# A dynamic convolution and a maxout layer in one kernel: first batch sooner, weights by halves, and w1 turned by the crossbar

## The chip, the cores and the metric

The kernel runs on one core of a Trainium2 chip. The metric is the device time of one execution in microseconds (us), lower is better. A time is some 1.8 us above the span of the profile (from the first to the last instruction): the profiled execution of the kernel before has a span of 429.9 us and a time of 431.71. TensorE does the matmuls; VectorE, ScalarE and GpSimd do the rest; SyncE, ScalarE and GpSimd issue transfers, which all run on the same 16 DMA engines.

## The reference

```python
# x (8, 4160, 192), weight_gen (8, 4160, 8 heads, 7 taps), w1, w2 (192, 1024), w_out (1024, 192), all fp32
w = exp(weight_gen - max);  w = w / (sum over the 7 taps + 1e-9)
conv[b, s, h, :] = sum over k of w[b, s, h, k] * x_padded[b, s + k, h, :]     # 24 features a head
out = maximum(conv @ w1, conv @ w2) @ w_out                                    # 33280 tokens
```

The kernel uses max(a, b) = a + relu(b - a). So it needs wd = w2 - w1 for the hidden product, and w10 = w1 @ w_out once, to add conv @ w10 to the output.

## The kernel before

The tokens lie as 128 partitions x 260 columns of 192 features. Batches of 16 columns go through ScalarE (exponentials) and VectorE (seven tap products, then adds). The result must be transposed for TensorE, in units of 4 or 8 columns. A unit of four columns in the opening is summed and transposed on TensorE (`sum_transpose`: 6 blocks x 7 taps, 42 matmuls); later units are added on VectorE and transposed by the DMA crossbar (`transpose`). The hidden product runs in groups of two tiles at first and of three tiles from tile 12 on.

```python
def transpose(u):                        # VectorE has added; the crossbar transposes
    ...
    nc.sync.dma_start_transpose(out=yt[...], in_=y_ts[b][:, o * D:(o + n) * D])

def sum_transpose(u):                    # TensorE adds the seven taps and transposes
    ...
    for k in range(nb):
        for t in range(K):
            nc.tensor.matmul(yps[:, k * P:(k + 1) * P], lhsT=m_ts[b][...], rhs=ident,
                             start=(t == 0), stop=(t == K - 1), skip_group_check=True)
    nc.scalar.copy(out=yt[:, 0:nb * P], in_=yps[:, 0:nb * P])

# opening (cut): four whole weight loads on one queue, then
load_x(0, 4, 4); load_x(0, 8, 4); ...    # GpSimd, behind the landing of w1's first piece
keep_warm(110)                           # filler matmuls
w1_transposed()                          # 24 transposes on TensorE
keep_warm(6)
sum_transpose(0)
...
tensor_tensor(out=wd["E"], ...)          # VectorE: 1024 features at once, with all three copies
mul(0, 4); red(1); mul(0, 8)
hidden(0); ln(1); hidden(1)
sum_transpose(1)
...                                      # pw: the product w10, 24 matmuls
# and by groups: sum_transpose(2) to (5), transpose(6) on
```

The softmax here doesn't subtract the row's maximum and nothing guards it: scores larger than these inputs give would overflow.

Of the kernel before, what the change touches and what calls it, by code (L numbers as in the profile page):

```python
# [23 lines left out]
def kernel(  # L24
# [107 lines left out]
    def ln(b):  # L132
        nc.scalar.activation(out=s_ts[b], in_=s_ts[b], func=AF.Ln)

    def shift(b):
        TH = BATCHES[b][1] * H
        nc.vector.tensor_tensor(
            out=_sub(wg_ts[b], 0, [[K, TH], [1, K]]),
            in0=_sub(wg_ts[b], 0, [[K, TH], [1, K]]),
            in1=_sub(s_ts.pop(b), 0, [[1, TH], [0, K]]), op=ALU.subtract,  # L140
        )
# [169 lines left out]
    for t0, n in GROUPS:  # L311
        most = 2 if len(OUTS) < 10 or len(OUTS[-1]) == 4 else 4
        OUTS.append([])
        while len(OUTS[-1]) < most and c < NT:
            u = column(c)[0]
            if TILES.index((u, 0)) + UNITS[u][2] > t0:
                break
            OUTS[-1] += [c, c + 1]
            c += 2
    OUTS.append(list(range(c, NT)))  # L320
    NU = len(UNITS)

# [14 lines left out]
    def stretch(g):  # L337

        if g < len(GROUPS):
            t0, n = GROUPS[g]  # L340
            for t in range(t0, t0 + n):
                for f in chunks(t)[0]:
                    for j in range(2):
                        hid_rest(t, f, j, t == t0 + n - 1)
        for k in range(0, len(OUTS[g]), 4):
            if g == len(GROUPS) and k < 8:
                tag, w = ("ab", 2048) if k == 0 else ("c", 1024)
                tile_, at = ps[tag].tile([P, w], FP32, name="op_" + tag, tag=tag), 0
            else:
                tile_, at = ps["r" if "r" in ps else "o"].tile([P, 1024], FP32, name="op_ps", tag="op"), 0  # L350
            for c in OUTS[g][k:k + 4]:
                op_at[c // 2] = tile_, at + (c - OUTS[g][k]) // 2 * D
                out_rest(c, c - OUTS[g][k] < 2)
# [25 lines left out]
    with tc.tile_pool(name="pstage", bufs=1) as pstage:  # L379
# [17 lines left out]
        for wi, wsrc in enumerate((moe_w1, moe_w2)):  # L397
            for kind, r0, nr in (("E", 0, P), ("T", P, 64)):
                nc.sync.dma_start(
                    out=ws[kind, wi],  # L400
                    in_=bass.AP(tensor=wsrc.tensor, offset=r0 * F, ap=[[F, nr], [1, F]]),
                )
# [15 lines left out]
        weights(0, 0)  # L418
        nc.scalar.copy(out=xb_ts[0][:, PAD * D:(PAD + 4) * D], in_=xs[:, PAD * D:])  # L419
# [3 lines left out]
        for kind in "ET":  # L423
            nc.scalar.copy(out=w1[kind], in_=ws[kind, 0])
        for o in (4, 8, 12):
            weights(0, o)

        nc.gpsimd.tensor_copy(out=gate, in_=ws["E", 0][:, 0:1])
        load_x(0, 4, 4)
        load_x(0, 8, 4)  # L430
        nc.gpsimd.dma_start(
# [3 lines left out]
        load_x(0, 12, 4)  # L435
# [6 lines left out]
        tp = ps["o"].tile([P, 1024], FP32, name="tp", tag="op")  # L442
        tpb = tp[:, :].bitcast(BF16)

        def w1_transposed():

            for fi in range(FCH):
                for at, kind, nr in ((0, "E", P), (P + 64, "E", 64), (P, "T", 64)):
                    nc.tensor.matmul(  # L449
                        tpb[:, fi * 256 + at:fi * 256 + at + nr],  # L450
                        lhsT=w1[kind][0:nr, fi * P:(fi + 1) * P],
                        rhs=ident[0:nr, 0:nr], is_transpose=True, skip_group_check=True,
                    )
# [3 lines left out]
        def keep_warm(times):  # L457

            for _ in range(times):
# [3 lines left out]
        keep_warm(110)  # L463
        w1_transposed()
        nc.scalar.copy(out=w1t[:, 0:1024], in_=tpb[:, 0:1024])
        keep_warm(6)
        sum_transpose(0)
        nc.scalar.copy(out=w1t[:, 1024:2048], in_=tpb[:, 1024:2048])
        exp_sum(1)
        keep_warm(18)  # L470

        nc.vector.tensor_tensor(out=wd["E"], in0=ws["E", 1], in1=ws["E", 0], op=ALU.subtract)
        nc.vector.tensor_copy(out=wd["R"][64:P, :], in_=wd["E"][0:64, :])
        nc.vector.tensor_copy(out=wd["O"][0:64, :], in_=wd["E"][64:P, :])
        nc.vector.tensor_tensor(out=wd["R"][0:64, :], in0=ws["T", 1], in1=ws["T", 0],
                                op=ALU.subtract)
        nc.vector.tensor_copy(out=wd["O"][64:P, :], in_=wd["R"][0:64, :])
        mul(0, 4)
        red(1)
        mul(0, 8)  # L480


        hidden(0)
        ln(1)
        hidden(1)
        sum_transpose(1)
        shift(1)
        weights(1, 0)
        weights(1, 4)
        mul(0, 12)  # L490


        pw = ps["o"].tile([P, 1024], FP32, name="pw", tag="op")
        for k in range(3):
            for fi in range(FCH):
                nc.tensor.matmul(  # L496
                    pw[:, k * 256:k * 256 + D],
                    lhsT=w1t[:, fi * 256 + 64 * k:fi * 256 + 64 * k + P],
                    rhs=wo[:, fi * D:(fi + 1) * D],
                    start=(fi == 0), stop=(fi == FCH - 1), skip_group_check=True,  # L500
                )
        nc.scalar.copy(out=_sub(w10, 0, [[D, 3], [1, D]]), in_=_sub(pw, 0, [[256, 3], [1, D]]))
# [4 lines left out]

    def first_of_1():
        m_ts[1] = m_ts[0]
        mul(1, 0)  # L510
        load_x(2, 0, 16)
        load_wg(4, nc.gpsimd)

    def rest_of_1():
        shift(2)
        mul(1, 8)
        load_wg(5, nc.gpsimd)
        load_x(3, 0, 16)
        red(3)
        adds(1, 8)  # L520
# [4 lines left out]
        2: (lambda: (first_of_1(), exp_sum(2), sum_transpose(2)), lambda: weights(1, 8)),  # L525
        3: (lambda: (red(2), ln(2), mul(1, 4), exp_sum(3), sum_transpose(3)), rest_of_1),
        4: (lambda: sum_transpose(4), lambda: weights(2, 0)),
        5: (lambda: (ln(3), sum_transpose(5)), lambda: (exp_sum(4), transpose(6))),
# [3 lines left out]
    def extra(t):  # L532
# [4 lines left out]
        if s == 0 and b + 1 < NB:  # L537

            c = b + 1
            if c + 1 < NB:  # L540
                shift(c + 1)
            if c + 2 < NB:
                red(c + 2)
            for o, _ in pieces(c):
                mul(c, o)
                adds(c, o)
            if b + 5 < NB:
                load_wg(b + 5, nc.gpsimd)
            if b + 3 < NB:
                load_x(b + 3, 0, BATCHES[b + 3][1])  # L550
        if k == 2 and 6 < u + 1 < NU:
            transpose(u + 1)
        if b + 2 < NB:
            for o, at in zip((o for o, _ in pieces(b + 2)), (6, 9)):
                if s == at:
                    weights(b + 2, o)
        if s == 3 and b + 3 < NB:
            ln(b + 3)
        if s == 0 and b + 4 < NB:
            exp_sum(b + 4)  # L560

    for g in range(2, len(OUTS)):
        if GROUPS[min(g, len(GROUPS) - 1)][1] == 3 and "c" not in ps:
            later_ps()
        hidden(g)
# [7 lines left out]
        for k in range(0, len(OUTS[g]), 4):  # L573
            now = OUTS[g][k:k + 4]
# [38 lines left out]
```

## Time and profile before

| kernel before | |
|---|---|
| time, median of 3 | 431.97 us (431.97 to 432.0) |
| span, granted clock | 429.9 us, 1.000 |
| TensorE busy | 420.8 us, 98% |
| VectorE, ScalarE busy | 378.8 us (88%), 351.5 us (82%) |
| first useful hidden matmul | 17.38 us |
| first group of three tiles | 47.82 us |
| last copy of outputs starts | 425.39 us |

The three last rows cut the span into opening, first stretch, steady part and tail; a change in one of them is read from how far the next row moves. TensorE's waits before, from the waits view (line and tensor, what ended the wait, us in total, times, the longest), show how little there was to lose after the start:

```profile
PE hdp L228 <- ACT rd_t L247: 1.0, 1, 1.0
PE op_ps L266 <- ACT o_t L296: 0.4, 1, 0.4
```

After the start, one relu and one copy are waited for, once each, and a second relu for 0.2 us; no DMA is. The list of DMA issues of the same kernel (KB left out for a transpose; median us from issue to landing):

```profile
yt<-y_t SPq DMA_TRANSPOSE x30, 4.5
```

### The profile page before, as it was taken

The page shows a single profiled execution, that of the slowest core. Times are in us where ns is not written, and L with a number is a line of the kernel's source. Part 1 is how long each engine was busy: PE and PEld are TensorE (multiplying, and loading weights), DVE is VectorE, ACT ScalarE, POOL GpSimd, SP SyncE. Part 2 cuts the span into 40 slices and gives each one's busy share as a digit, 9 for nine tenths or more (in the row PEclk, how much of TensorE's full clock was granted, in tenths as well). Part 3 has the DMA queues.
Part 4 walks back from the last instruction along what each step waited for, and adds up shares of the span by engine and source line. Part 5 has one row for each costly group of instructions (what it writes and reads, how often), then busy time and mean ns, then how long its engine had stood idle before and what let it go on. Part 6 is the DMA issues. An engine that isn't in the chain of part 4 may idle for free.

```text
span 429.9 us, 9266 instructions
## 1 busy us (share of the span) xinstructions
PE 420.8 (98%) x4186; PEld 302.8 (70%) x4186; DVE 378.8 (88%) x170; ACT 351.5 (82%) x351; POOL 29.8 (7%) x61
## 2 busy tenths in 40 slices
PE   7999999999999999999999999999999999999995
PEld 7699886767677676676666766667767677676785
DVE  4998999999999999999999999999999999992000
ACT  6777898888889888897988888888878887777762
POOL 2221001010000101010100101010000000000000
PEclk9999999999999999999999999999999999999999
DMA  8984837667482858576392948558565736433112
GB/s 266 206 184 173 176 103 147 161 153 212 121 231 50 211 149 210 126 166 199 50 311 78 208 121 215 114 118 215 131 139 164 148 102 157 104 107 104 75 75 110
DMA packets 59047, 65.45 MB, mean 152 GB/s; under 512 B 48865, under 2 KB 49633, under 8 KB 59008
## 3 DMA queue, kind: packets, MB, share of 16 engines
q0 software_dynamic: 6400, 24.30, 25.7%
q1 hardware_dynamic: 47280, 15.00, 19.0%
q10 hardware_dynamic: 5328, 25.56, 14.8%
q8 instruction: 32, 0.52, 0.5%
q14 instruction: 7, 0.06, 0.0%
HBM read 35.96 MB, written 25.56 MB: 143 GB/s over the span
## 4 chain that ended last, share of the span: by engine, by line
PE 95%; ACT 4%; issue 0%; DVE 0%; ACTq 0%; POOL 0%; POOLq 0%
PE op_ps L283 38%; PE hd L228 26%; PE hd L238 14%; PE op_ps L273 5%; PE yps L199 3%; PE op_ps L266 2%; PE warm L460 2%; ACT rd_t L247 2%; PE hdp L228 1%; PE hdp L238 1%; ACT e_t L125 1%; PE op_c L283 1%; PE op_ab L283 1%; PE tp L449 1%; ACT o_t L296 0%; PE pw L496 0%
## 5 line engine op out<-in xcount | busy, mean ns | idle before, releaser
L247 ACT ACTIVATE rd_t<-hd 128x2048 bf16<-128x2048 f32 (+1 forms) x166 | 230.8, 1443 | 34.1 <-PE hd L238 33.7
L283 PE MATMUL op_ps<-wo,rd_t 128*128 128x192 bf16 x2016 | 194.2, 246 | 0.0
L159 DVE TENSOR_TENSOR m_t<-xb_t,en_t 128x10752 bf16<-128x10752 bf16 (+1 forms) x36 | 187.3, 5206 | 1.5 <-ACT xb_t L419 1.4
L283 PEld LDWEIGHTS <-rd_t 128*128 128x128 bf16 x2080 | 175.6, 98 | 9.2
L228 PE MATMUL hd<-yt,wdE 128*128 128x512 bf16 (+1 forms) x264 | 96.5, 369 | 0.2 <-ACT rd_t L247 0.2
L228 PE MATMUL hd<-yt,wdO 128*128 128x512 bf16 (+1 forms) x264 | 95.5, 366 | 0.0
L177 DVE TENSOR_TENSOR m_t<-m_t 128x4608 bf16<-128x4608 bf16 (+1 forms) x30 | 75.5, 2517 | 1.0
L296 ACT COPY o_t<-op_ps 128x768 f32<-128x768 f32 (+1 forms) x87 | 54.5, 626 | 20.0 <-PE op_ps L283 19.8
L238 PE MATMUL hd<-yt,wdR 64*128 64x512 bf16 (+1 forms) x528 | 68.0, 366 | 0.0
L273 PE MATMUL op_ps<-w,yt 128*128 128x192 bf16 x252 | 62.0, 246 | 0.0
L178 DVE TENSOR_TENSOR m_t<-m_t 128x3072 bf16<-128x3072 bf16 (+1 forms) x30 | 51.9, 1731 | 1.0
L238 PEld LDWEIGHTS <-wdR 64*128 64x128 bf16 x576 | 20.9, 94 | 44.9 <-issue 35.3
L228 PEld LDWEIGHTS <-wdE 128*128 128x128 bf16 x288 | 28.0, 97 | 28.9 <-issue 19.3
L228 PEld LDWEIGHTS <-wdO 128*128 128x128 bf16 x288 | 28.3, 98 | 11.3 <-issue 1.5
L148 ACT ACTIVATE en_t<-wg_t 128x896 bf16<-128x896 f32 (+1 forms) x36 | 34.1, 955 | 2.1 <-ACT o_t L296 2.1
L273 PEld LDWEIGHTS <-yt 128*128 128x128 bf16 x260 | 25.4, 98 | 9.3 <-issue 0.2
L113 POOL DMA_DIRECT2D xb_t<-in_x_dram x20 | 10.8, 544 | 292.5 <-DVE m_t L159 292.5
L179 DVE TENSOR_TENSOR y_t<-m_t 128x1536 bf16<-128x1536 bf16 (+1 forms) x30 | 28.3, 945 | 1.0
L266 PE MATMUL op_ps<-w,yt 64*128 64x192 bf16 x252 | 24.6, 243 | 0.4 <-ACT o_t L296 0.4
L266 PEld LDWEIGHTS <-yt 64*128 64x128 bf16 x260 | 12.7, 94 | 14.6 <-issue 0.7
L130 DVE TENSOR_REDUCE sum_t<-e_t 128x128 f32<-128x896 f32 (+1 forms) x17 | 17.7, 1039 | 3.2 <-ACT e_t L125 3.0
L125 ACT ACTIVATE e_t<-wg_t 128x896 f32<-128x896 f32 (+1 forms) x17 | 15.6, 919 | 4.9 <-ACT o_t L296 2.5
(55 smaller groups left out, 158.2 us busy)
## 6 DMA issues: line engine op xcount, KB each, us to landing
out_dram<-o_t ACTq DMA_DIRECT2D x29, 768.0 KB, 3.3
xb_t<-in_x_dram POOLq DMA_DIRECT2D x14, 768.0 KB, 7.4
wg_t<-in_weight_gen_dram POOLq DMA_DIRECT2D x14, 448.0 KB, 8.0
xb_t<-xb_t POOLq DMA_DIRECT2D x16, 288.0 KB, 8.0
out_dram<-o_t ACTq DMA_DIRECT2D x6, 384.0 KB, 3.7
wg_t<-in_weight_gen_dram SPq DMA_DIRECT2D x2, 448.0 KB, 6.5
xb_t<-in_x_dram POOLq DMA_DIRECT2D x4, 192.0 KB, 6.4
xb_t<-in_x_dram POOLq DMA_DIRECT2D x2, 384.0 KB, 7.6
```

Of the source, the lines that this page charges most:

```text
L148: nc.scalar.activation(out=_sub(en_ts[b], o * WGC * 2, [[2 * N, K], [2, N], [1, 2]]), in_=_sub(wg_ts[b], o * WGC, [[1, K], [K, N], [0, 2]] ...
L159: nc.vector.tensor_tensor(out=m_ts[b][:, K * o * D:K * (o + n) * D], in0=_sub(xb_ts[b], o * D, [[D, K], [1, n * D]]), in1=_sub(en_ts[b], o ...
L177: nc.vector.tensor_tensor(out=taps(0, 1, 3), in0=taps(0, 1, 3), in1=taps(3, 1, 3), op=ALU.add)
L178: nc.vector.tensor_tensor(out=taps(0, 2, 2), in0=taps(0, 2, 2), in1=taps(1, 5, 2), op=ALU.add)
L179: nc.vector.tensor_tensor(out=y_ts[b][:, o * D:(o + w) * D], in0=taps(0, 1, 1), in1=taps(2, 1, 1), op=ALU.add)
L228: nc.tensor.matmul(hid_out(t, f, j), lhsT=wd[kind][:, f * P:(f + 1) * P], rhs=_sub(yt_ts[u], 2 * j * P, [[3 * P, w // P], [1, P]]), start= ...
L238: nc.tensor.matmul(hid_out(t, f, j), lhsT=wd["R"][r, f * P:(f + 1) * P], rhs=_sub(yt_ts[u][r, :], P, [[3 * P, w // P], [1, P]]), start=fir ...
L247: nc.scalar.activation(out=rd[:, k * 1024:(k + n) * 1024], in_=hd[:, at:at + n * 1024], func=AF.Relu)
L266: nc.tensor.matmul(op_out(c), lhsT=yt_ts[u][r, (3 * i + 1) * P:(3 * i + 2) * P], rhs=w10[r, 2 * D:3 * D], start=first, stop=False, skip_gr ...
L273: nc.tensor.matmul(op_out(c), lhsT=yt_ts[u][:, (3 * i + 2 * j) * P:(3 * i + 2 * j + 1) * P], rhs=w10[:, j * D:(j + 1) * D], start=False, s ...
L283: nc.tensor.matmul(op_out(c), lhsT=rd[:, k * 1024 + at:k * 1024 + at + P], rhs=wo[:, f * D:(f + 1) * D], start=False, stop=(f == FCH - 1), ...
L296: nc.scalar.copy(out=_sub(o_t[0], (k + 2 * q) % 24 * D, [[2 * D, w], [D, 2], [1, D]]), in_=_sub(tile_, at + q * D, [[D, w], [512, 2], [1, ...
```

## The change

Its intent: let hidden work begin earlier, by loading and subtracting half of the features first and by taking the 24 w1 transposes off TensorE (the crossbar does them later, just for w10); and sum five units instead of six on TensorE. The order of VectorE's and ScalarE's work in the first groups, the filler, the steady part's order and the tail (last columns as 4, 2, 2) change with it. Its core:

```diff
+        HF = F // 2
+        def load_w(h):
             for kind, r0, nr in (("E", 0, P), ("T", P, 64)):
+                for wi, wsrc in enumerate((moe_w1, moe_w2)):
+                    nc.sync.dma_start(out=ws[kind, wi][:, h * HF:(h + 1) * HF], in_=...)
+        load_w(0)
+        load_w(1)
 ...
-        nc.gpsimd.tensor_copy(out=gate, in_=ws["E", 0][:, 0:1])
+        nc.gpsimd.tensor_copy(out=gate, in_=wg_ts[0][:, 0:1])
         load_x(0, 4, 4)
+        nc.gpsimd.tensor_copy(out=gate[0:64, :], in_=ws["T", 1][:, 0:1])
         load_x(0, 8, 4)
 ...
         def w1_transposed():
-            for fi in range(FCH):
-                for at, kind, nr in ((0, "E", P), (P + 64, "E", 64), (P, "T", 64)):
-                    nc.tensor.matmul(tpb[...], lhsT=w1[kind][...], rhs=ident[...], is_transpose=True, ...)
+            for at, kind, nr in ((0, "E", P), (P + 64, "E", 64), (P, "T", 64)):
+                nc.sync.dma_start_transpose(
+                    out=_sub(w1t, at, [[256, FCH], [1, nr]]), in_=w1[kind][0:nr, :])
 ...
+        w_diff(0); sum_transpose(0); keep_warm(14); w_diff(1); mul(0, 4)
+        hidden(0)
+        nc.scalar.copy(out=w1["E"], in_=ws["E", 0])
+        mul(0, 8); sum_transpose(1); mul(0, 12)
+        nc.vector.tensor_copy(out=w1["T"], in_=ws["T", 0])
+        w1_transposed()
+        hidden(1)
 ...
+        hidden(2)
+        ...                      # mul(1, 0), sum_transpose(2), load_x(2, ...), load_wg(4, ...)
+        adds(1, 4); transpose(5)
+        hidden(3); w10_product(); sum_transpose(3)
```

## The prediction

> **What bounds the kernel now.** I read the page's chain first, because it says which engine has to become faster for the end to move.
>
> ```profile
> ## 4 chain that ended last, share of the span: by engine, by line
> PE 95%; ACT 4%; issue 0%; DVE 0%; ACTq 0%; POOL 0%; POOLq 0%
> ```
>
> The chain is TensorE almost throughout. So I cut the span into stretches and asked for each engine's busy time in each (columns: stretch, its length, then busy time and instruction count of PE, PEld, DVE, ACT, POOL, the granted clock, the DMA share and GB/s).
>
> ```profile
> 3.00:11.20 8.20, 8.18 (x112) 8.08 (x112) 4.05 (x3) 5.64 (x8) 2.20 (x5) 1.00 1.04 331
> 11.20:17.38 6.18, 6.18 (x91) 5.32 (x90) 6.04 (x7) 3.37 (x6) 1.00 (x2) 1.00 1.26 224
> 17.38:47.82 30.44, 29.45 (x414) 26.11 (x411) 28.73 (x14) 24.04 (x32) 5.37 (x10) 1.00 0.71 173
> 47.82:400.00 352.18, 351.63 (x3304) 242.73 (x3303) 338.33 (x144) 301.81 (x291) 19.76 (x37) 1.00 0.60 151
> ```
>
> From 47.82 us on, where the groups of three tiles begin, TensorE is idle for 0.55 us of 352: nothing can be won there unless matmuls go. Between 17.38 (the first useful hidden matmul) and 47.82 it is idle for 1.0 us of 30.4. Before 17.38 it looks busy too, but most of that is filler. So a gain must come from three places: a start before 17.38, fewer matmuls before 47.82, or the tail. The chain in order of time (start, length, what) shows the start:
>
> ```profile
> 3.02 8.19 PE warm L460 x110
> 11.20 2.51 PE tp L449 x24
> 13.71 0.44 PE warm L460 x6
> 14.15 2.36 PE yps L199 x42
> 16.53 0.80 ACT yt L205
> 17.33 0.91 ACT w1t L468
> 18.25 0.85 ACT e_t L125
> 19.10 0.92 ACT rd_t L247
> ```
>
> The first unit's summing transpose (yps, 42 matmuls) ends at 16.5, ScalarE copies it, hidden work starts at 17.38, and the second group then waits because ScalarE still does a w1 copy and the next exp before its relu. What the 14.15 itself waits for is on VectorE (timeline: start, length, engine, line, operation):
>
> ```profile
> 9.33 2.96 DVE L159 TENSOR_TENSOR m_t<-xb_t,en_t 128x5376 bf16<-128x5376 bf16 x1 [1.40 <-ACT xb_t L419]
> 12.21 1.22 DVE L472 TENSOR_TENSOR wdE<-ws1E,ws0E 128x1024 bf16<-128x1024 f32 x1
> 14.35 1.22 DVE L475 TENSOR_TENSOR wdR<-ws1T,ws0T 64x1024 bf16<-64x1024 f32 x1
> 16.05 2.96 DVE L159 TENSOR_TENSOR m_t<-xb_t,en_t 128x5376 bf16<-128x5376 bf16 x1
> ```
>
> The product of the first four columns ends at 12.3, yet its summing waits until 14.15 behind the 24 w1 transposes on TensorE. The tail, from the timeline:
>
> ```profile
> 424.53 0.82 PE L283 MATMUL op_c<-wo,rd_t 128*128 128x192 bf16 x8
> 425.39 0.80 ACT L296 COPY o_t<-op_c 128x768 f32<-128x768 f32 x1 [2.17 <-PE op_c L283]
> 426.22 0.82 ACTq L303 DMA_DIRECT2D out_dram<-o_t  x2
> ```
>
> After the last matmul come a copy of four columns (0.80), two output issues (0.82) and the landing.
>
> **What the Trainium skill says.** "TensorE: Matmul & The Clock Gate", section "Back-to-back issue gap", gives N/2.4 + 2.5 ns between warm matmuls, 55.8 ns for 128 columns, but about 81 ns in a real stream with weight loads. The trace decides for the first: 42 summing matmuls take 2.35 us, 56.0 ns each, so a whole unit's summing costs TensorE 2.35 us. The same page, "What's actually happening", says an idle window of some 3.4 us halves the clock; the trace grants 1.00 everywhere, and the new filler has to keep gaps shorter than that. "VectorE: DVE Perf Modes", "The perf-mode tier table", has fp32 tensor_tensor at 1 element a cycle and an fp32 copy at 2; with its (N+151)/0.96 the 1024-wide subtraction should take 1.22 us, exactly the trace's, so I take 0.69 us for a half of 512 as an estimate, and some 0.56 us for the 768-wide copy that moves to VectorE. "DMA: Bandwidth & Descriptors", "Issuing engines are not separate DMA queues", says that all queues share the 16 DMA engines; the trace agrees as far as it goes: a DMA share of about 1.0 or more until 17.4 us, so moving a load ahead only delays another.
>
> **The change part by part.**
>
> *Start.* VectorE's first shift ends at 7.93 as now. The x cast goes to VectorE (about 0.6, to 8.5) and the first weights are done at 8.57 on ScalarE, so the first product runs about 8.65 to 11.6, 0.7 us earlier. TensorE no longer transposes w1 there. Its filler (40, then 40 pairs on half the rows, which overlap, then 15) ends by my estimate between 10 and 12, so summing runs 11.65 to 14.05 instead of 14.15 to 16.5. VectorE meanwhile subtracts half the features: 0.69 for E to 12.3, 0.69 for R to 12.9. The three half-width copies are now ScalarE's, about 0.6 each by its 0.54 us spacing for 448 elements: they end at about 14.1. The weight bytes are no limit: the first half is 0.79 MB where the whole is 1.57, and even the second tensor of the old order had landed by 12.2. ScalarE's yt copy then runs to 14.95, hidden work starts at about 15.1: **2.3 us earlier**. Only tiles with features of the first half are in the first group, so the second half's subtractions (to about 14.5) and copies (14.95 to 16.7) are off this path.
>
> *Five units instead of six on TensorE.* Minus 42 matmuls, **2.35 us**. VectorE takes over the adds of a four-column unit: half of 2.55 + 1.76 + 0.96, some 2.6 us, and a DMA transpose (4.5 us median to landing). It is needed by tile 20, near 50 us, and lands by my walk near 42.
>
> *w1 by the crossbar.* The 24 transposes stood in time that had no useful work for TensorE, so removing them is already in the start. What is added is a path: ScalarE casts w1E after the first relus (about 18.5 to 19.5), VectorE casts w1T after four products (14.5 + 3 x 2.9 = 23.3, to 23.9), then landing. With 4.5 us it is there at 28.5; the product w10 comes up at about 28.3 and needs the T part only after its first eight matmuls (0.66 us). So nearly no wait, or up to 3 us if the transpose is slow.
>
> *New waits between 15.1 and group six.* Walking the order of the instructions: after hidden group 0 (1.7 us, to 16.8) the next sum waits for the product of columns 4 to 7, which ends at about 17.4: 0.7. Groups 1 and 2 wait for relus, 0.25 and 0.3. ScalarE then stands at the logarithm of batch 1, whose sum waits for VectorE's products until about 24.9, so relus of group 2 run 25.2 to 27.1 and group 3 waits some 0.45. w10's wait 0.3. Together 2.0 to 2.7 us, where before it was 1.0: **1.3 us given back**. Starting from 29.4 of useful work, 15.1 + 29.4 - 2.35 + 2.35 = 44.5 for the start of the three-tile groups, against 47.82: 3.3 earlier.
>
> *Steady state.* Same matmuls, so the same 9.01 us per six tiles (in the chain, the first hidden matmuls of every second group are 9.01 us apart). VectorE's sixteen-column batch takes 24.1 us against TensorE's 24.04, so it must not fall behind. In the old trace the first eight-column transpose is issued at 48.5 and needed at about 66; in the new one I find about 49.4 and 62. The lead shrinks from some 13 to 8 us after the 4.5 us landing, and stays positive.
>
> *Tail.* The last eight columns leave as 4, 2 and 2: a copy of two columns (0.48 instead of 0.80) and one issue instead of two (0.4 less). **0.7 us.**
>
> Sum: -2.3 - 2.35 + 1.3 - 0.7 = -4.05 us, so 431.97 - 4.05 = 427.9 us, a ratio of 0.991.
>
> **The rivals.** First, VectorE takes over as the bound: it is 88% busy, has no idle time after 50 us, and gets 2.6 us of adds while TensorE comes 3.3 us earlier. For it speaks the near equality 24.1 to 24.04; against it the 8 us of lead. If it held, TensorE would lose what exceeds the lead, and the time would be 429 to 431. Second, w1's crossbar path or the bunching on ScalarE costs more than I walked: a w1t landing of 7.7 us (the slowest DMA transpose of the old trace) makes w10 wait 2.9 more, and the time 430.5. Third, the waits were tuned away and the gaps before group six stay at 1 us: then 426.6. Fourth, the loads bound the start, with the second x piece now asked for before the weights: a first half 1.5 us late would stop the subtractions and give 429.
>
> **Range and chances.** The three sizes that I trust (2.3, 2.35, 0.7) sum to 5.35, so 426.6 is about the best, and I take 0.4 off for the roundness of the walk: 426.2. The rivals reach 430.5; I cut the range just under the last, at 430.3. The 2% mark lies at 423.3, beyond everything that I can add up, and slower needs several microseconds of new waits twice over: 2% faster, 97% same, 1% slower.
>
> **What would show it.** Right: hidden matmuls start near 15.1; five yps blocks of 42; the three-tile groups start near 44.5; no wait of TensorE on yt after that; the last copy is 0.48 us with one issue behind it. Wrong: a TensorE wait on a w1t or yt transpose, a VectorE wait for ScalarE's logarithm in the steady part, a granted clock under 1.00 after the pause before the first sum, or hidden work that starts after 16.

## The result, and the profile after

| | before | after |
|---|---|---|
| time, median | 431.99 us (431.97 to 433.07, 4 runs) | 446.06 us (443.69 to 456.43, 4 runs) |
| fast runs | all | 443.69, 444.69, 447.44 |
| span, clock of the profiled run | 429.9 us, 1.000 | 445.6 us, 0.975 |
| first useful hidden matmul | 17.38 | 15.24 |
| first group of three tiles | 47.82 | 64.88 |
| last copy starts, end of span | 425.39, 429.9 | 441.94, 445.6 |

The ratio is 1.0301, with a 95% interval of 1.0242 to 1.036: 3% slower, where a gain of 1% was predicted. Ratios here are the mean time of one kernel's fast runs over that of the other's of the same rounds, so not quite the ratio of the medians that I quote. The run of 456.43 us (clock 0.966) isn't used for the ratio; it does stand in the median and range of the table (the median of the three fast runs is 444.69). The trace is of the run of 447.44 us, the slowest of the three.

The chain that ended last, by engine:

```profile
PE 88%; DMA 7%; ACT 3%; DVE 1%; issue 0%; POOL 0%; DVEq 0%
```

DMA, absent from the list of before, now carries 7% of the path, some 31 of 445.6 us. The stretches (columns as in the prediction: stretch, length, busy time and count of PE, PEld, DVE, ACT, POOL, granted clock, DMA share, GB/s) say where:

```profile
3.00:15.24 12.24, 10.91 (x192) 10.41 (x193) 8.18 (x8) 7.23 (x12) 3.92 (x7) 1.00 1.05 277
15.24:64.88 49.64, 32.77 (x368) 27.70 (x368) 31.21 (x16) 24.84 (x33) 5.38 (x10) 0.79 0.87 125
64.88:417.00 352.12, 351.92 (x3310) 243.48 (x3310) 340.73 (x146) 301.35 (x292) 19.78 (x37) 1.00 0.64 152
```

The start came earlier, as intended, and the steady part is as full as before (TensorE idle 0.2 us of 352). All the loss is in the stretch between: 49.64 us long instead of 30.44, with TensorE idle for 16.87 us of it, and its clock at 0.79. TensorE's waits name three of them:

```profile
PE pw L519 <- DMA w1t<-w1T: 6.6, 1, 6.6
PE pw L519 <- DMA wg_t<-in_weight_gen_dram: 6.2, 1, 6.2
PE yps L197 <- DVE m_t L157: 4.7, 2, 3.5
```

`pw` is the product w10. The first of its waits to end is put down to a weight_gen load, which w10 doesn't read. No such load lands near 38.6 us, where the matmul starts, but the first transpose of w1E does (20.02 + 18.56 = 38.58), and the view of w1t puts a 6.5 us wait of the weight load down to it; so w1t is what was waited for. What these waits do to the work behind them is in TensorE's timeline (start, length, operation, count, wait ahead of it and its releaser):

```profile
20.40 4.15 PE L197 MATMUL yps<-ident,m_t 128*128 128x128 bf16 x42 [3.48 <-DVE m_t L157]
...
38.62 1.46 PE L519 MATMUL pw<-wo,w1t 128*128 128x192 bf16 x8 [6.22 <-DMA wg_t<-in_weight_gen_dram]
46.66 2.74 PE L519 MATMUL pw<-wo,w1t 128*128 128x192 bf16 x16 [6.58 <-DMA w1t<-w1T]
49.20 3.58 PE L197 MATMUL yps<-ident,m_t 128*128 128x128 bf16 x42
```

The waits are 3.48, 6.22 and 6.58 us. And the sum of 42 blocks behind a wait takes 4.15 or 3.58 us where it took 2.51 in every place before; the 24 matmuls of w10 take 4.20 us together, 2.14 before. In these microseconds the granted clock is 0.50 (22 to 24 us, and 36 to 50 us). The chain in order of time says what was waited for (start, length, what):

```profile
8.58 8.71 DMA xb_t<-in_x_dram
17.38 2.97 DVE m_t L157
...
26.70 19.92 DMA w1t<-w1T
```

The x columns 4 to 7, asked for at 8.58, land at 17.3, so VectorE multiplies them from 17.38 and the second sum starts at 20.40. The last w1 transpose is asked for at 26.70 and lands 19.92 us later, four times the usual. (The two of w1E took 18.6 and 23.4 us.) These are not three independent measurements: the second was asked for while the first was under way and landed at 44.90, and the third, asked for behind both on the same queue, landed at 46.62. How much of its 19.92 us is its own isn't shown. Who issues at that time? SyncE's queue, then GpSimd's:

```profile
20.02 5.13 SPq L472 DMA_TRANSPOSE w1t<-w1E  x2
26.70 6.84 SPq L472 DMA_TRANSPOSE w1t<-w1T  x1
```

```profile
20.14 0.56 POOL L103 DMA_DIRECT2D wg_t<-in_weight_gen_dram  x1
20.68 0.57 POOL L113 DMA_DIRECT2D xb_t<-in_x_dram  x1
21.20 0.58 POOL L103 DMA_DIRECT2D wg_t<-in_weight_gen_dram  x1
26.37 0.54 POOL L113 DMA_DIRECT2D xb_t<-in_x_dram  x1 [4.59 <-DVE m_t L157]
```

Each transpose falls within a few tenths of a microsecond of a load that GpSimd issues, and SyncE is held 6.84 us by a single transpose. From 28 to 38 us the 16 DMA engines have a busy share of 1.49 and move 47 GB/s; from 17 to 24 they moved 232 at a share of 1.15. The engines are occupied, not loaded. In the tail, the last copy is of two columns with one issue behind it:

```profile
441.94 0.48 ACT L294 COPY o_t<-op_ps 128x384 f32<-128x384 f32 x1 [1.01 <-PE op_ps L281]
442.45 0.34 ACTq L301 DMA_DIRECT2D out_dram<-o_t  x1
```

From its start to the end of the span it is 3.66 us, against 4.5 before.

### The profile page after: what moved, and what is told of

It reads as the page before. It is cut to its first block, busy times and chain, and to the rows that moved or that the text cites. A ratio compares the mean times of both kernels' runs of the same rounds, so it can differ in the third digit from the quotient of the medians.

```text
span 445.6 us, 9193 instructions
## 1 busy us (share of the span) xinstructions
PE 420.5 (94%) x4135; PEld 301.4 (68%) x4135; DVE 381.8 (86%) x174; ACT 349.9 (79%) x352; POOL 30.5 (7%) x62
## 4 chain that ended last, share of the span: by engine, by line
PE 88%; DMA 7%; ACT 3%; DVE 1%; issue 0%; POOL 0%; DVEq 0%
PE op_ps L281 38%; PE hd L226 26%; PE hd L236 14%; PE op_ps L271 5%; DMA w1t<-w1T 4%; PE op_ps L264 3%; PE yps L197 2%; DMA xb_t<-in_x_dram 2%; ACT rd_t L245 1%; DMA wg_t<-in_weight_gen_dram 1%; DVE m_t L157 1%; PE pw L519 1%; ACT en_t L146 0%; ACT o_t L294 0%; DVE wg_t L138 0%; DVE sum_t L130 0%
## 5 line engine op out<-in xcount | busy, mean ns | idle before, releaser
L281 PE MATMUL op_ps<-wo,rd_t 128*128 128x192 bf16 x2080 | 200.2, 246 | 0.0
L175 DVE TENSOR_TENSOR m_t<-m_t 128x4608 bf16<-128x4608 bf16 (+1 forms) x31 | 76.9, 2480 | 1.1
L294 ACT COPY o_t<-op_ps 128x384 f32<-128x384 f32 (+1 forms) x89 | 56.1, 630 | 25.9 <-PE op_ps L281 23.8
L271 PE MATMUL op_ps<-w,yt 128*128 128x192 bf16 x260 | 64.0, 246 | 0.0
L176 DVE TENSOR_TENSOR m_t<-m_t 128x3072 bf16<-128x3072 bf16 (+1 forms) x31 | 52.9, 1706 | 1.1
L226 PEld LDWEIGHTS <-wdO 128*128 128x128 bf16 x288 | 28.3, 98 | 10.8 <-issue 1.1
L138 DVE TENSOR_TENSOR wg_t<-wg_t,sum_t 128x896 f32<-128x896 f32 (+1 forms) x17 | 17.8, 1044 | 13.8 <-ACT sum_t L133 13.8
L113 POOL DMA_DIRECT2D xb_t<-in_x_dram x20 | 10.8, 541 | 223.4 <-DVE m_t L157 223.4
L264 PEld LDWEIGHTS <-yt 64*128 64x128 bf16 x260 | 12.8, 94 | 14.6 <-issue 0.7
```

The costliest lines, as they stand in the source:

```text
L175: nc.vector.tensor_tensor(out=taps(0, 1, 3), in0=taps(0, 1, 3), in1=taps(3, 1, 3), op=ALU.add)
L176: nc.vector.tensor_tensor(out=taps(0, 2, 2), in0=taps(0, 2, 2), in1=taps(1, 5, 2), op=ALU.add)
L226: nc.tensor.matmul(hid_out(t, f, j), lhsT=wd[kind][:, f * P:(f + 1) * P], rhs=_sub(yt_ts[u], 2 * j * P, [[3 * P, w // P], [1, P]]), start= ...
L264: nc.tensor.matmul(op_out(c), lhsT=yt_ts[u][r, (3 * i + 1) * P:(3 * i + 2) * P], rhs=w10[r, 2 * D:3 * D], start=first, stop=False, skip_gr ...
L271: nc.tensor.matmul(op_out(c), lhsT=yt_ts[u][:, (3 * i + 2 * j) * P:(3 * i + 2 * j + 1) * P], rhs=w10[:, j * D:(j + 1) * D], start=False, s ...
L281: nc.tensor.matmul(op_out(c), lhsT=rd[:, k * 1024 + at:k * 1024 + at + P], rhs=wo[:, f * D:(f + 1) * D], start=False, stop=(f == FCH - 1), ...
```

## The experiments

The questions: why do the w1 transposes take 20 us (their layout, rows of 64 or 128 elements written 512 bytes apart; or their company, the loads issued beside them); what do the waits, the half clock, the x load and the fifth unit each cost? "Group six" is the first group of three tiles; its start sums up the opening. All complete kernels gave correct results, and medians and ranges in the table are of all runs, the ratios of fast runs alone (one run of the changed kernel and one of after_apart were slow). Each trace is of one execution: the fastest for after_apart, best4 and best6, the slowest fast one for the changed kernel, xbar_contig, before_xbar, best3 and best5.

| kernel | median us (range, runs) | ratio to before | group six at |
|---|---|---|---|
| before | 431.99 | | 47.82 |
| after | 446.06 (443.69 to 456.43, 4) | 1.0301 | 64.88 |
| undo_xbar | 437.31 (436.96 to 439.08, 4) | 1.0126 | 48.25 |
| xbar_contig | 438.24 (437.75 to 439.21, 4) | 1.0142 | 56.66 |
| before_xbar | 433.16 (431.69 to 438.06, 4) | 1.0010 | 54.36 |
| undo_xearly | 434.99 (431.73 to 436.74, 4) | 1.0034 | 47.10 |
| undo_six | 434.11 (432.98 to 435.36, 4) | 1.0024 | 50.47 |
| after_warm | 441.15 (440.63 to 442.63, 4) | 1.0192 | 58.83 |
| after_apart | 436.39 (433.18 to 443.01, 4) | 1.0060 | 48.00 |
| best1 | 431.37 (430.52 to 434.33, 4) | 0.9981 | 49.82 |
| best3 | 433.33 (431.13 to 437.41, 4) | 0.9997 | 45.85 |
| best4 | 433.07 (431.31 to 437.05, 6) | 1.0028 | 45.49 |
| best5 | 431.69 (430.31 to 432.44, 6) | 0.9971 | 49.29 |
| best6 | 431.39 (430.23 to 434.18, 6) | 0.9979 | 47.16 |

### micro: transposes measured by themselves

A kernel that holds nothing but crossbar transposes, each waited for (wrong result): every layout twice alone, then three of them with loads of GpSimd beside them.

```diff
+variant("y12" + r, [(128, 12, 128)])                                # as yt
+variant("e8p" + r, [(128, 8, 256)])                                 # as w1t's E part
+variant("h8p" + r, [(64, 8, 256)])                                  # as w1t's 64-row parts
+variant("all" + r, [(128, 8, 256), (64, 8, 256), (64, 8, 256)])
+variant("y12x", [(128, 12, 128)], loads=3)                          # with x loads from GpSimd
```

> Wrong result on purpose: only transposes, one at a time on a DMA system with nothing else in it, each waited for before the next. Theory L (layout): the w1 transposes are slow in themselves, because blocks land 512 bytes apart (pitch 256) or because only 64 rows are transposed. Then the pitch-256 or the 64-row variants take over 10 us from issue to landing even alone, the contiguous 128-row ones of 12 and 8 blocks under 5. Theory C (contention): a transpose alone takes under 5 us in every form, about in proportion to its blocks, and only the three variants beside three x loads of 1.5 MB each take over 10 us.

Alone, the twelve blocks of a yt transpose land in 3.7 us, w1t's 128-row part in 3.1 (3.0 written contiguously) and a 64-row part in 2.7; all three in a row take 5.4 us. Beside an x load issued 0.16 us after it, the twelve-block transpose took 19.7 us, in the same kernel on the same chip. With the load 2.5 and 2.7 us ahead, the w1t shapes took 5.3 and 4.7. So the layout isn't the cause; company is, and only at some distances in time.

### undo_xbar: the changed kernel with w1 transposed on TensorE

```diff
-                nc.sync.dma_start_transpose(out=_sub(w1t, at, ...), in_=w1[kind][0:nr, :])
+                    nc.tensor.matmul(tpb[...], lhsT=w1[kind][...], rhs=ident[...], is_transpose=True, ...)
+            nc.scalar.copy(...)  # two halves
         nc.vector.tensor_copy(out=w1["T"], in_=ws["T", 0])
-        w1_transposed()
 ...
         hidden(2)
+        w1_transposed()
```

> The changed kernel with w1 transposed on TensorE again (after hidden group 2) and nothing else undone. If the crossbar path is the loss, both waits of the w10 product (6.2 and 6.6 us) and the half-clock stretch behind them (some 3 us) go, 2.5 us of transposes and some ScalarE copies come back: 446 - 12.8 - 3 + 2.5 = about 432 to 434, still with the wait of 3.5 us for the product of columns 4 to 7. The rival, that the slow clock or the crowded start is the cause whatever w1 does, expects over 440.

Some 7.6 us of the loss go (the means of the fast runs are 445.27 and 437.67), less than the 12 to 14 that I expected. The waits of w10 are gone and group six starts at 48.25. But the kernel is still 1.3% slower than before, and the trace has a wait that the changed kernel had been too late to show:

```profile
68.25 0.61 PE L226 MATMUL hd<-yt,wdE 128*128 128x512 bf16 x1 [4.47 <-DMA yt<-y_t]
```

That is the first eight-column transpose: issued at 52.86, landed 15.3 us later, with a weight_gen load issued 1.0 us behind it (and 14.1 us under way itself). The clock falls to 0.66 from 64 to 70 us.

### xbar_contig: the w1 transposes in yt's own shape

```diff
-              for kind, nr in (("E", P), ("T", 64))}
+              for kind, nr in (("E", P), ("Y", P), ("X", P))}      # rows put together on VectorE first
+            for k, kind in enumerate("EYX"):
+                nc.sync.dma_start_transpose(out=w1t[k][:, :].rearrange(...), in_=w1[kind][:, :])
```

> The changed kernel with three transposes of 128 rows into three tiles without gaps between blocks, in place of one of 128 and two of 64 rows into blocks 512 bytes apart (four more small copies on VectorE build the sources, about 1.5 us). Theory L: landing falls from about 20 to about 5 us and the time to 430 to 435. Theory C: landing stays over 15 us and the time at 444 or more.

Landing took 10.1, 10.8 and 10.2 us and w10 waited 4.7: between the expectations, a fit for neither. The shape alone doesn't cure it. The moments of issue moved as well: two of the transposes stood at 27.75 and 29.04, beside GpSimd's issues at 28.54 and 29.07, and SyncE was held 5.10 us by the last.

### before_xbar: the kernel before with nothing but the crossbar for w1

```diff
 def w1_transposed():
-            ...24 transposes on TensorE, and two copies of ScalarE
+                nc.sync.dma_start_transpose(out=_sub(w1t, at, [[256, FCH], [1, nr]]), in_=w1[kind][0:nr, :])
```

> The kernel before with only the w1 transposes moved to the crossbar. If the crossbar path alone is the loss, the product w10, which comes up at 24 us, waits until the third transpose lands: issued at about 11, 20 us or more each when slow, so at 35 to 45, and the time becomes 443 to 455. If the crossbar is slow only in the changed kernel's order, it lands by 24 and the time stays within 1 us of 432.

The same in time (interval 0.9982 to 1.0038), with a wide spread: 431.69, 432.2, 434.12 and 438.06. So the crossbar for w1 cost this kernel nothing that can be told from the noise. In the profiled run, the longest of them, the transposes took 9.8 to 16.1 us, again amid GpSimd's issues (transposes at 10.54 to 14.77, loads at 9.48 to 11.98), and w10 waited 3.9 and 1.5. So the transposes can be slow in the old order too; the three faster runs were not traced.

### micro2: the distance in time between a transpose and a load

One transpose of 128 x 1536 and one load of 16 columns of x, with the load's issue moved against that of the transpose; once each from GpSimd with and without a cast, and from ScalarE (wrong result).

```diff
+for b, a in ((6,0), (4,0), (2,0), (1,0), (0,0), (0,1), (0,2), (0,4), (0,6)):  # pauses before, behind
+    variant(..., b, a, "pool")        # GpSimd, with a cast
+variant(..., "poolf")                 # GpSimd, without
+variant(..., "act")                   # ScalarE's queue
```

> Wrong result on purpose: one 128x1536 transpose and one 1.5 MB x load per variant, nothing else under way, the load asked for at set times before or after the transpose. Theory C1 (any overlap): whenever both are in flight, both slow, so every variant from 4 us before to 4 us after takes over 10 us. Theory C2 (order): only a load asked for by GpSimd at the same time as the transpose or within its 3 us behind it drags both to 15 to 20 us, as in the 19.7 us seen; a load asked for 2 us or more ahead leaves the transpose at 5 us or less, as in the 5.3 and 4.7 seen. For the same load asked for by ScalarE, theory C3 (the software queue is the cause) expects under 8 us in every order; if ScalarE's is as slow, the queue is not the cause.

The chain of this kernel in order of time, each line one transpose from issue to landing:

```profile
20.60 4.62 DMA p<-src
...
50.84 7.10 DMA p<-src
...
82.79 17.53 DMA p<-src
...
187.33 19.07 DMA f<-src
```

| load issued, against the transpose | -4.55 | -3.1 | -1.65 | -0.92 | +0.33 | +0.94 | +1.67 | alone |
|---|---|---|---|---|---|---|---|---|
| landing of the transpose, GpSimd with cast, us | 4.6 | 5.3 | 7.1 | 8.1 | 17.5 | 5.6 | 3.7 | 3.7 |

Without the cast it is 19.1 us at +0.33 and 5.4 at -3.1, so the cast plays no part. From ScalarE's queue at +0.13 it is 8.3 us (4.2 at -3.6), over double the time alone, just over the 8 that the milder theory allowed. At +0.33 both transfers crawl (the load took 18.6 us): the DMA engines have a share of 0.67 and move 67 GB/s in those 17.5 us. VectorE is busy for 0.02 us of them, so no compute engine is needed for it. In this bench, with one execution of each distance, a transpose and a GpSimd load issued 0.33 us behind it hold each other up for some 12 to 15 us; 1.67 us behind, the load costs the transpose nothing, and 1.65 us ahead still 3.4 us.

### undo_xearly: the x load asked for first

From undo_xbar, with the load of columns 4 to 7 issued at 4.6 us.

```diff
+        load_x(0, 4, 4)
         exp_sum(0)
 ...
-        nc.gpsimd.tensor_copy(out=gate, in_=wg_ts[0][:, 0:1])
-        load_x(0, 4, 4)
```

> As the run with w1 on TensorE (437.3), with the load of x columns 4 to 7 asked for as soon as the first weight batch has landed, about 4.8 us, where it was about 8.6. If that load's lateness holds up the second product (2.3 us of VectorE's wait, 2.0 of TensorE's), it starts at about 15 and not 17.4 and the time falls by 1.5 to 2.5 us, to 435 to 436. Rival: the load only takes the bandwidth of the weights, whose first half then comes later by the same, and the time stays at 437 or rises.

VectorE's second product starts at 14.90 without a wait, TensorE waits 1.03 us there instead of 2.05, and the median falls by 2.3 us (from another round on another chip; the ratio to before falls from 1.0126 to 1.0034). The wait on the eight-column transpose stays, at 2.85. The range of 5 us among these runs makes the size uncertain; the place isn't.

### undo_six: the sixth unit on TensorE again

```diff
-        adds(1, 4)
-        transpose(5)
 ...
-        5: (none, lambda: transpose(6)),
+        5: (lambda: sum_transpose(5), lambda: transpose(6)),
```

> As the run with w1 on TensorE (437.3), with six units summed on TensorE again, so without the transpose of unit 5 and 2.6 us of adds on VectorE. If the 4.5 us wait for the transpose of unit 6 (landing 15.3 us) and the half clock after it come from VectorE's shift, they go, and 2.35 us of matmuls come back: 437.3 - 4.5 - 3 + 2.35 = about 432. If the slow landing has nothing to do with the sixth unit, the time rises to 439 or more.

TensorE works 2.3 us more before group six (32.56 against 30.31 us) and the kernel is 3.2 us faster by the medians (ratio 1.0024 against 1.0126, again another round): no wait on yt is left, and no yt transpose takes over 7.1 us. The first one now has no load issued within 3 us of it and lands in 6.9 us instead of 15.3, so this run doesn't separate the lead from the company. A unit on TensorE has a fixed price; one taken off it moves everything closer to the landing of the transposes.

### after_warm: the changed kernel with its waits filled

```diff
+        for _ in range(fill):            # 58 filler matmuls before the sum of unit 1
+            nc.tensor.matmul(yps[:, 0:P], lhsT=ident, rhs=ident, ...)
+                for _ in range((100, 110, 0)[k]):      # in the two waits of w10
```

> The changed kernel with filler matmuls in its three long waits (58 before the second sum, 100 and 110 inside the w10 product), nothing else. If the half clock behind the waits is a cost of its own, the sum of unit 1 (4.15 us), the product (some 4.2 us in its two parts) and the sum of unit 3 (3.58) go back to 2.5, 2.1 and 2.5 us: 4 to 5 us less than the changed kernel, so 441 to 442. If the clock costs nothing, the time stays at 444 to 447.

The filler stands for 3.40, 5.75 and 6.30 us, where the waits were 3.48, 6.22 and 6.58, and nothing waits behind it. The filler's length is fixed by its count, so the waiting time is nearly the same by design, 0.8 us less, but the clock is 1.00 throughout; the sums take 2.52 and w10 2.30 us, and group six starts 6.05 us earlier. Some 5 us of the loss are the half clock by itself. (The transposes landed in 8.9 and 10.5 us here, though issued at nearly the same moments, 20.15 and 26.55, beside loads at 20.03 to 21.09 and 26.22. One order changed: the first transpose stands 0.12 us behind a load here, and 0.12 us ahead of one in the changed kernel.)

### after_apart: the crossbar kept, but apart from the loads

```diff
-            for at, kind, nr in ((0, "E", P), (P + 64, "E", 64), (P, "T", 64)):
+            for at, kind, nr in ((P, "T", 64), (0, "E", P), (P + 64, "E", 64)):    # 23 to 25 us, in one row
-        mul(0, 12)
         nc.vector.tensor_copy(out=w1["T"], in_=ws["T", 0])
+        mul(0, 12)
 ...
+        for at in (0, P, P + 64):                      # GpSimd's next loads wait for the landing
+            nc.gpsimd.tensor_copy(out=gate, in_=w1t[:, at:at + 1])
         load_x(2, 0, 16)
```

> The changed kernel with its three crossbar transposes of w1 kept, but asked for in one row once both sources are cast (about 24 us, two to three us after GpSimd's loads), and GpSimd's next loads held until the three have landed. If it is the coincidence with a load asked for by GpSimd in the same microsecond that makes a transpose take 20 us, landing falls to 5 to 9 us, the w10 product waits under 3 us and the time is 430 to 436. If any loads in flight do it, landing stays over 12 us and the time over 440.

The same three transposes land in 4.5 (median of the two of E) and 6.4 us (T), SyncE is held at most 2.23 us by one, w10 doesn't wait, and group six starts at 48.00 instead of 64.88. Its queue:

```profile
23.04 2.23 SPq L472 DMA_TRANSPOSE w1t<-w1T  x1
25.37 3.30 SPq L472 DMA_TRANSPOSE w1t<-w1E  x2
```

GpSimd's nearest issues are at 20.53 and 31.42. The transposes' shapes, queue and bytes are those of the changed kernel; their order and their distance from those issues are new. The loads of 19.47 to 20.53 us are still under way then (landing at 24.89 to 28.81), so loads in flight alone don't do it. So in the kernel itself, too, it is the company at the issue, though order and distance were changed together. What is left above the kernel before: the x load (wait of 2.78, then the sum at half clock, 3.58 us) and a wait of 2.46 on the eight-column transpose. That transpose took 12.9 us, with a weight_gen load 0.60 us behind it.

### best1, best3 and best4: putting the findings together

best1 takes no crossbar for w1, but does the w1 transposes on TensorE in two halves inside the filler, with six units and the early x load. best3 and best4 keep the crossbar and five units, with the loads behind it held until it lands; best4 also issues each weight_gen load right behind the x load, some 4 us ahead of the next transpose.

```diff
 # best1, from undo_six
+        load_x(0, 4, 4)                                # early
+        w1_transposed(0)  ...  hidden(0);  w1_transposed(1)
 # best3, from after_apart
+        load_x(0, 4, 4)                                # early
+        for kind in "ET":                              # w1 cast by halves on ScalarE
+            nc.scalar.copy(out=w1[kind][:, 0:HF], in_=ws[kind, 0][:, 0:HF])
+                nc.gpsimd.tensor_copy(out=gate, in_=yt_ts[6][:, 0:1])   # one load held behind yt(6)
 # best4, from best3
-                nc.gpsimd.tensor_copy(out=gate, in_=yt_ts[6][:, 0:1])
-                load_wg(b + 5, nc.gpsimd)
                 load_x(b + 3, 0, BATCHES[b + 3][1])
+                load_wg(b + 5, nc.gpsimd)
```

> No crossbar transpose before unit 6: w1 on TensorE by halves in two gaps, six units summed on TensorE, the x load early; kept of the change: softmax and weights by halves, tail. From 434.1 of the run with six units, minus about 2 for the x load and 1.5 for the gaps: 430 to 431, a little under the kernel before. If the start gains nothing in truth, 432 or more.

> The changed kernel's plan with its collisions taken out: x load early, w1 cast by halves on ScalarE, its three crossbar transposes in one row at about 20 us with GpSimd's next loads held until they land, and GpSimd's load of batch 6 held behind the transpose of unit 6; five units. If the collisions and the late x load were all that was wrong with the plan, the three-tile groups start near 44.5 to 46 and the time is 427 to 429.5, as predicted for the change. If five units and the crossbar cost something besides, 431 or more.

> As the last kernel with its collisions at the start taken out (433.3, with waits of 5.3 and 1.0 us on transposes in the steady part), with every load of a weight batch asked for right behind the x load, so always some 4 us ahead of the next transpose. If those waits were coincidences of a weight load with a transpose, no transpose lands later than 9 us, TensorE waits for none, and the time is 427 to 429 in nearly all executions. If a shrunken lead of VectorE alone is the cause, the waits stay and the time is 431 to 435.

best1 is level with the kernel before (interval 0.9936 to 1.0026), and none of the three reaches the time expected of it. best3 and best4 start group six at 45.85 and 45.49, two microseconds before the old kernel, near the predicted 44.5: the opening can do what I had worked out. But they give it back later, waiting on yt in the steady part: 5.3 us at 162 in best3 (a transpose of 14.9 us beside a weight_gen load of 13.5), and 1.6 and 1.1 us in best4. There the slow transposes (10.6 and 11.2 us) were issued 0.9 and 1.6 us ahead of an output store of ScalarE. That the store does it isn't shown: in the kernel before, a store 0.07 us behind the first transpose left it at 5.3 us, and in best4 itself others at 0.2 and 1.7 us left it at 5.8 and 7.3. best4's lead from issue to need is 7.7 to 12 us; in the kernel before it is 15.3 for the first and 10.7 to 14 later.

These kernels also narrow what company means. Their w1T transposes are issued behind a load, 0.80 us (best3), 0.22 (best4) and 0.59 (best5), and land in 4.7, 5.5 and 5.3 us. Over all traces, eight of the nine transposes that took over 12 us with no other transpose under way had a GpSimd load issued 0.12 to 1.01 us behind them; the ninth is best5's at 147.09 us, 12.4 us with no issue within 3 us, in company of three loads asked for 4 to 5 us ahead. A load close behind isn't enough either (5.6 us at 0.94 in the bench, 9.8 to 10.8 in xbar_contig and before_xbar). No experiment changed the order alone.

### best5 and best6: six units, and the last wait filled

```diff
 # best5, from best4
-        adds(1, 4)
-        transpose(5)
+        5: (lambda: sum_transpose(5), lambda: transpose(6)),
 # best6, from best5
-        sum_transpose(1)
+        sum_transpose(1, 28)                           # 28 filler matmuls ahead of it
```

> The same with six units summed on TensorE. Five units save TensorE 2.35 us if VectorE's lead holds, so this one should be about 2.3 us slower than its neighbour, 429.5 to 431.5; if the lead is what is short, it is as fast or faster.

> The six-unit version with the crossbar kept apart, plus 28 filler matmuls on TensorE in the wait ahead of the sum of unit 1 (about 1.6 us of work in a wait that was 2.04 us in the slower executions). Theory: what separates its 430.3 us executions from its 431.1 to 432.4 us ones is the half clock behind that wait (sum of 42 blocks 4.14 us instead of 2.5); with the wait filled nearly all executions read 430 to 430.8, granted clock 1.0, sum of unit 1 at 2.5 us, ratio to before 0.994 to 0.996. Rival: the spread comes from the landing of the crossbar transposes of the steady part, and the filler changes nothing: 430.3 to 432.4 again, ratio 0.997; if the filler delays the sum, 431 to 433.

best5 is the only version whose interval lies below 1: 0.3% faster than the kernel before (0.9948 to 0.9994), far under the 2% that would count as faster. Its executions differ, 430.31 us twice at clock 1.000, 431.06 at 0.999, and 432.3 to 432.4 three times at 0.994 to 0.995. The profiled one is of the second kind and shows a half clock behind a short wait, 2.04 us:

```profile
18.91 4.14 PE L197 MATMUL yps<-ident,m_t 128*128 128x128 bf16 x42 [2.04 <-DVE m_t L157]
```

The length of the wait alone doesn't decide it: 2.05 us (undo_xbar) and 2.25 us (undo_six) at the same place cost no half clock, 1.11 us in best1 did. In every trace the granted clock changes on a grid of 3.41 us steps, fixed within the run. Over the 14 traces of complete kernels, the tail aside, each full-clock step in which TensorE was busy for at most 1.45 us, ten in all, was followed by half clock, and each with 1.58 us or more by full clock, but for one, best1's step at 17.18 us (2.30 us busy, 1.2 of them w1 transposes). In best5 the whole wait falls into one step (columns as before; `prof best5 --windows 16.08:19.50,19.50:22.91`):

```profile
16.08:19.50 3.42, 1.38 (x21) 0.90 (x16) 3.42 (x2) 3.37 (x6) 1.08 (x2) 1.00 1.41 204
19.50:22.91 3.41, 3.41 (x36) 3.41 (x34) 3.41 (x2) 0.52 (x2) 0.00 (x0) 0.50 0.96 267
```

In undo_six the border of a step at 17.50 us cuts the wait in two, and the emptier of the two steps still has 1.58 us of work.

best6 fills that wait. In its profiled execution the sum takes 2.51 us, group six starts at 47.16 instead of 49.29, the clock is 1.000 and the time 430.23. But the other five read 431.24 to 434.18 at clocks of 0.998 to 1.000, so the expectation that nearly all would be near 430.3 fails. The half clock fits best5's two kinds of execution, of which one was traced; what spreads best6's isn't shown, since only its fastest was traced. (In the same rounds the kernel before spread from 431.62 to 435.89.)

## Why the prediction was wrong

The predicted and measured terms, in us, with TensorE's work at full clock taken from best4 (27.90 us busy in the same stretch, with 369 matmul records against the changed kernel's 368; 27.05 is 44.5 - 15.1 less the midpoint 2.35 of the predicted waits):

| term | predicted | measured | difference |
|---|---|---|---|
| first useful hidden matmul | 15.1 | 15.24 | +0.1 |
| TensorE's work from there to group six | 27.05 | 27.90 | +0.9 |
| wait ahead of the second sum | 0.7 | 3.48 | +2.8 |
| waits of w10 | 0.3 | 12.80 | +12.5 |
| other waits (rest of the midpoint 2.35) | 1.35 | 0.59 | -0.8 |
| half clock (32.77 - 27.90) | 0 | 4.87 | +4.9 |
| **group six starts** | **44.5** | **64.88** | **+20.4** |
| from there to the end of the span | 381.4 | 380.7 | -0.7 |

- **Start: right.** 15.24 against 15.1. The half-width loads and subtractions did what was worked out, and in every kernel built on the changed one the start lies between 15.1 and 15.6.
- **w1 by the crossbar: the step that failed.** "With 4.5 us it is there at 28.5 ... So nearly no wait, or up to 3 us if the transpose is slow." The landing was 18.6 to 23.4 us, and with it went 12.8 us of waits. I took the duration from the transposes of the old trace, 2.8 to 7.7 us, and my second rival took the slowest of them for the worst. But none of those 30 is issued within 2.5 us of a load that GpSimd issues: I compared the issue times afterwards, and the nearest two are 2.58 us apart. They were no sample of the place where the new ones stand. The two benches and after_apart show that not the shape mattered but the loads that GpSimd issued close by, within some tenths of a microsecond in the bench. I had worked out when the transposes would be asked for, and never when the loads would.
- **Waits between 15.1 and group six: one term mis-sized.** "The next sum waits for the product of columns 4 to 7, which ends at about 17.4: 0.7." The product only began at 17.38, as its x load took 8.7 us amid the weights. I had written that moving a load ahead only delays another, and did not apply it to this one; the fourth rival looked for the delay in the weights, and it fell on x. undo_xearly shows it: asked for at 4.6, the product starts at 14.90.
- **Half clock: named as a sign, left out of the sum.** 4.9 us, which after_warm confirms with its 6.05 us earlier group six, of which 0.8 are shorter waits. A wait of TensorE that leaves a clock step with 1.45 us of work or less costs more than itself.
- **Five units instead of six: right on TensorE, wrong as a gain.** 2.3 us of TensorE's work do go (undo_six: 32.56 against 30.31). "The lead shrinks from some 13 to 8 us after the 4.5 us landing, and stays positive" fails on the same landing: 15.3 us in undo_xbar. (The reading behind it was off too: the old trace first uses that transpose at 63.80 us, not about 66, so the lead was 10.8 us, not 13.) Not VectorE, as the first rival had it, but the transpose ate the lead. In the changed kernel this stayed unseen, because TensorE came 17 us late anyway.
- **Steady state and tail: right.** TensorE is as full as before from group six on. Behind the last copy 0.85 us were won, against 0.7.
- **Range and chances.** Each rival had one delay with a size from the old trace. Their sums were loose as well: 427.9 + 2.9 is 430.8, not 430.5, and the first rival reached 431, yet the range was cut at 430.3. The failure was of a size outside that trace, and it brought the half clock with it; 1% for slower was far too sure for a change that put three transfers at a place where none had been.

What stays open: what inside the DMA engines makes a transpose and a load hold each other up, whether the order of load and transpose is what decides, how much of the third w1 transpose's 19.9 us was its own (with a load at the same distance it took 10.5 us in after_warm, where the two ahead of it landed at 29.5 and 30.1 us and not at 38.58 and 44.90), and what spreads the executions of best6. Distances between -0.9 and +0.1 us were not measured in the benches.

## What to carry to other kernels

Before a transfer goes on the critical path, look at which other transfers will be issued in the same microsecond, and place it a few microseconds away from them, above all from a load right behind it; this helped in after_apart but is no guarantee (best5's 12.4 us). A median landing time from another part of the trace says nothing about that. Price a new TensorE wait by the clock steps that it empties: in these traces a step of 3.41 us with 1.45 us of work or less made the next one run at half clock. And where an engine is made to come earlier, check the lead of every asynchronous producer against its slowest landing, not its median.

## What the Trainium skill lacked or had wrong

- "DMA: Bandwidth & Descriptors", section "Rules for kernel authors": "A transpose next to ordinary DMAs needs nothing." The row is on corruption, and there the runs agree: every complete kernel was correct. For time they don't: 3.7 us alone, 17.5 and 19.1 us beside a load issued by GpSimd 0.33 us later, 8.3 us beside one of ScalarE at 0.13 us, and 18.6 to 23.4 us in the changed kernel.
- The same page, section "Issuing engines are not separate DMA queues", has all queues interleave on the same engines. It lacks that a transpose and a load together can move far less than either alone: 47 GB/s at a DMA share of 1.49 from 28 to 38 us, against 232 GB/s just before.
- "TensorE: Matmul & The Clock Gate", section "What's actually happening": the clock halves after an idle window of some 3.4 us, with free-running windows. The traces agree on the windows: the clock changes on a grid of 3.41 us steps. They don't agree that the window has to be idle: 1.45 us of work or less in it was enough for the half clock in ten steps, as in best5, where a wait of 2.04 us was followed by a sum of 4.14 us instead of 2.51. With 1.58 us or more of work the clock stayed full, but for one step in best1. A limit of 3.4 us on single waits is too generous for these traces.
